# Sliding-window attention and hard-swish MLP: x^T of three pairs by DMA transposes, scores on other banks, and queries in another order

## The chip, the cores and the metric

The kernel runs on one core of a Trainium2 chip. The time is device microseconds of one execution; the median of 8 runs before the change is 320.78 us (319.51 to 322.16). Five engines with a queue each work beside one another: TensorE (PE), VectorE (DVE), ScalarE (ACT), GpSimd (POOL) and SyncE (SP), which here only issues DMAs. Each queue is worked through in order, so an instruction that waits holds up all that stand behind it on its engine.

## What is computed

Attention with 8 batches of 8 heads, 576 tokens and 64 dimensions, where a query sees itself and the 63 keys before it; its output, with the heads side by side, is the input x of 4608 tokens by 512 of two matrix products with a hard-swish between them.

```python
scores = scale * np.matmul(q, k.transpose(0, 1, 3, 2))
rel = pos[:, None] - pos[None, :]
mask = (rel >= 0) & (rel < 64)
attn = softmax(np.where(mask, scores, -1e9))
x = (attn @ v).transpose(0, 2, 1, 3).reshape(B * S, H * D)
h = x @ w_in                               # 4608 x 2048
g = h * np.clip(h + 3.0, 0.0, 6.0) / 6.0
out = g @ w_out                            # 4608 x 512
```

## The kernel before

**Tiles and stages.** The tokens are cut into nine tiles T of 512 for the matrix products, and into eight batches of 576 for attention. A stage is one tile. Its first half, `s1`, computes 16 chunks `fc` of 128 hidden columns: four matmuls (L452) into a PSUM bank, then the gate, an activation on ACT (L459) into a buffer `t` and a product on DVE (L460) into `gT`. Its second half, `s2`, has 16 slots of four matmuls (L489): four token blocks with four slots each, into the banks `o` and `acc` in turn; after the fourth slot of a block ACT copies the bank to `osb` (L495) and SP stores it (L498).

**Attention between the chunks.** In stage T attention of batch T + 1 is put between these, so that x of tile T + 1 is ready. The eight heads go as four pairs g. For a pair:

- `SS` (L551): scores of all key blocks in two PSUM banks `st0`, `st1` (ten matmuls, L347), two exponentials on ACT into `pT` (L355), and one product with the 0/1 mask on DVE, in place (`masked`, L365);
- `N_` (L534): P·V of both heads (L377 to L386), each into an `hT` bank, then for each head a reciprocal and a product on DVE into `opg` (L394, L397), which read that bank;
- `X_` (L539): five PE transposes of `opg` into an `hT` bank (L407) and an ACT copy into `xT` (L412), the x^T that `s1` of the next tile reads.

**What sets the order.** It is written out by hand. `stage_` (L698) runs a chunk or a slot and then the pieces that the tables `p1` (after a chunk of s1) and `p2` (after a slot of s2) of `pieces` (L716) give for its number. In tiles 2 to 6 pair 0's `SS` follows chunk 13, pair 1's slot 0, then `N_(0)` and `SS(2)` slot 3, and so on up to `X_(3)` after slot 14. Each engine receives its part in the order of these calls.

**Buffers.** `hT` has two banks (`ps_h`), which are taken in turn; `st0`, `st1`, `o` and `acc` are one each. `s1_bank` (L421) gives a chunk its bank: before, `hT` for the first two of every four chunks and `st0`/`st1` for the others, up to chunk 11; `o` and `acc` for 12 and 13; `hT` for 14 and 15. A bank is free again when the DVE product of its chunk, or the norm of its head, is done. `t` has three buffers (`t1pool`), `opg` two, and `pT` four.

**Loads and transposes.** `load_for_dma` (L124) brings Q, K and V of batch T + 2 in at the start of stage T, each as five DMAs on SP with rows of 256 bytes (L94). POOL casts them to bf16 (L252, L256, L243 to L247). `transpose_by_dma` (L264), called after slot 6, issues one DMA transpose each for Q and K on SP, into `QT` and `KT`, where a column is a token in order. For batch 2 this is done by pairs (L274), before tile 1. Batches 0 and 1 take another way, which stays.

Of the kernel before, what the change touches and what calls it, by code (L numbers as in the profile page):

```python
# [9 lines left out]
F32 = mybir.dt.float32  # L10
BF16 = mybir.dt.bfloat16
EXP = mybir.ActivationFunctionType.Exp
RELU = mybir.ActivationFunctionType.Relu
MULT = mybir.AluOpType.mult
# [10 lines left out]
def kernel(  # L25
# [9 lines left out]
    nc = tc.nc  # L35
    P = nc.NUM_PARTITIONS
    B, H, S, D = q.shape
# [4 lines left out]
    KB = (S + P - 1) // P  # L42
    SP = KB * P
    R = 4
    SM = P * R
    SR = S - SM
# [4 lines left out]
    QW = P + WINDOW  # L51
    VW = D + 1
    scale = 1.0 / math.sqrt(D)

    consts = ctx.enter_context(tc.tile_pool(name="consts", bufs=1))
    stage = ctx.enter_context(tc.tile_pool(name="stage", bufs=1))
    small = ctx.enter_context(tc.tile_pool(name="small", bufs=4))
    opool = ctx.enter_context(tc.tile_pool(name="opool", bufs=2))
    gpool = ctx.enter_context(tc.tile_pool(name="gT", bufs=1))
    t1pool = ctx.enter_context(tc.tile_pool(name="t1", bufs=3))  # L60
    t2pool = ctx.enter_context(tc.tile_pool(name="t2", bufs=2))
# [1 line left out]
    ps_st = ctx.enter_context(tc.tile_pool(name="ps_st", bufs=1, space=PSUM))  # L63
    ps_o = ctx.enter_context(tc.tile_pool(name="ps_o", bufs=1, space=PSUM))
    ps_h = ctx.enter_context(tc.tile_pool(name="ps_h", bufs=2, space=PSUM))
    ps_acc = ctx.enter_context(tc.tile_pool(name="ps_acc", bufs=1, space=PSUM))
# [56 lines left out]

    def load_for_dma(b):  # L124
        sts, ins = [], []
        for n, src in (("qst", q), ("kst", k), ("vst", v)):
            t = stage.tile([P, KB, H, D], F32, name=n, tag=n)
            ins += load_blocks(t, src, b, range(KB), SR if src is v else 0)
            sts.append(t)
        return tuple(sts), ins  # L130

    ctx.enter_context(tc.manual_schedule())
    def load_first():
# [24 lines left out]
    xT = consts.tile([P, NG, NT + SP - S], BF16, name="xT")  # L158
# [3 lines left out]
    def keep_busy(n):  # L162
# [11 lines left out]
        out=mask1[:], in_=mask1[:], pattern=[[1, QW]], compare_op=ISGE,  # L174
# [3 lines left out]
        out=mask1[:], in_=mask1[:], pattern=[[-1, QW]], compare_op=ISGE,  # L178
        fill=0.0, base=WINDOW - 1, channel_multiplier=1,
    )  # L180
    qn_all = consts.tile([P, NG, KB, 2, D], BF16, name="qn")
# [32 lines left out]
    fill_v(0)  # L214

    mask = consts.tile([P, 2 * (KB - 1), QW], BF16, name="mask")

    win16 = consts.tile([P, NG, FF], BF16, name="win16")
    wout16 = consts.tile([P, NFC, DM], BF16, name="wout16")
# [16 lines left out]
    class Batch:  # L236
# [10 lines left out]
            copy(out=self.V[SR:P, KB - 1, :, 0:D], in_=vst[SR:P, KB - 1, :, :])  # L247

        def cast_for_dma(self, st, which=(0, 1, 2)):
            for n, s in [((qn_all, st[0]), (kn_all, st[1]))[i] for i in which if i < 2]:  # L250
                for g in range(NG):
                    pcopy(  # L252
                        out=n[:, g, 0 : KB - 1, :, :].rearrange("p k h d -> p k (h d)"),
                        in_=s[:, 0 : KB - 1, 2 * g : 2 * g + 2, :].rearrange("p k h d -> p k (h d)"),
                    )
                pcopy(  # L256
                    out=n[:SR, :, KB - 1, :, :].rearrange("p g h d -> p g (h d)"),
                    in_=s[:SR, KB - 1, :, :].rearrange("p (g h) d -> p g (h d)", h=2),
                )
            if 2 in which:  # L260
                self.cast_v(st[2], 0, H, pcopy)
                self.cast_v_end(st[2], pcopy)
# [66 lines left out]
    def scores(bt, g, u, bias=False, bank=None):  # L329


        pT = P_ring[(bt.b * NG + g) % NPT]
        st = ps_st.tile([P, 2, 512], F32, name=f"st{u if bank is None else bank}")
        w = 2 * QW
        if bias:
            for h in range(2):
                nc.tensor.matmul(
                    st[:, h, 0:w], lhsT=ident[:], rhs=maskneg[:, u * w : (u + 1) * w],
                    start=True, stop=False,
                )  # L340
        blocks = (
            ((0, 0, 0, QW), (QW, P, P, QW)),
            ((0, 2 * P, 2 * P, QW), (QW, 3 * P, 3 * P, P), (QW + P, S - P, SM, SR)),
        )[u]
        for o0, k0, q0, n in blocks:
            for h in range(2):
                nc.tensor.matmul(  # L347
                    st[:, h, o0 : o0 + n],
                    lhsT=bt.KT[h * D : (h + 1) * D, g, k0 : k0 + P],
                    rhs=bt.QT[h * D : (h + 1) * D, g, q0 : q0 + n],  # L350
                    start=not bias, stop=not bias or o0 == blocks[-1][0],
                )

        def exps():
            nc.scalar.activation(  # L355
                out=pT[:, :, 2 * u : 2 * u + 2, 0:QW],
                in_=st[:, :, 0:w].rearrange("p h (k w) -> p h k w", k=2),
                func=EXP, scale=scale,
            )

        return exps

    def masked(bt, g):
        pT = P_ring[(bt.b * NG + g) % NPT]
        nc.vector.tensor_tensor(  # L365
            out=pT[:, :, :, 0:QW], in0=pT[:, :, :, 0:QW],
            in1=mask[:].rearrange("p (h k) w -> p h k w", h=2), op=MULT,
        )

    opgs = {}  # L370
# [41 lines left out]
        return lambda: acopy(out=xT[:, g, bt.b * S : (bt.b + 1) * S], in_=tr[:, 0:S])  # L412


    def h_bank():
        return ps_h.tile([P, 512], F32, name="hT")

# [3 lines left out]
    def s1_bank(fc, T):  # L421
        if T == 0:
            if fc in (6, 7):
                return (ps_o, ps_acc)[fc - 6].tile([P, 512], F32, name=("o", "acc")[fc - 6])[:]
            if fc in (8, 9, 12, 13):
                return ps_st.tile([P, 2, 512], F32, name=f"st{fc % 2}")[:, 0, :]
            return h_bank()[:]
        if fc in (12, 13):
            return (ps_o, ps_acc)[fc - 12].tile([P, 512], F32, name=("o", "acc")[fc - 12])[:]
        if fc % 4 < 2:  # L430
            return h_bank()[:]
        return ps_st.tile([P, 2, 512], F32, name=f"st{fc % 2}")[:, 0, :] if fc < 12 else h_bank()[:]
# [130 lines left out]
    bt, st = Batch(0), stage0  # L563
# [152 lines left out]
    def pieces(bt):  # L716
        if bt is None:
            return {}, {}
        f = lambda fn, *a: lambda: fn(bt, *a)
        p1, p2 = {}, {}  # L720
        p1 = {} if bt.b == 2 else {13: [f(SS, 0)]}
        p2 = {
            3: [f(N_, 0), f(SS, 2)], 5: [f(X_, 0)], 6: [f(N_, 1), f(SS, 3)],
            8: [f(X_, 1)], 9: [f(N_, 2)], 11: [f(X_, 2)], 12: [f(N_, 3)], 14: [f(X_, 3)],
        }
        if bt.b == 2:
            p2[0], p2[1] = [f(SS, 0)], [f(SS, 1)]
        else:
            p2[0] = [f(SS, 1)]
        return p1, p2  # L730

    bt2 = Batch(2)
    bt2.cast_for_dma(st2, (0, 1))
    for u0, osb in held:
# [4 lines left out]
    for T in range(1, NTB):  # L739
        p1, p2 = pieces(nxt)  # L740
        b = T + 2
        nxt = None
        if b < B:
            sts, _ = load_for_dma(b)
            nxt = Batch(b)
            p1.setdefault(12 if T == 1 else 6, []).append(
                lambda bt=nxt, sts=sts: bt.cast_for_dma(sts)
            )
            p2.setdefault(6, []).append(lambda bt=nxt: bt.transpose_by_dma())
        stage_(T, None, p1, p2)  # L750


# [28 lines left out]
```

## Time and profile before

Times of one profiled execution, in us. A row of DVE or ACT gives the mean of one instruction.

| what | value |
|---|---|
| time of the profiled execution, its span | 320.5, 318.8 |
| tiles 2 to 6, from start to start (95.5, 128.4, 161.2, 194.1, 227.0, 259.8) | 32.87 each |
| tiles 7 and 8, without attention | 27.63 each |
| PE transposes of x^T, L407 (160) | 14.2 busy |
| product with the mask on DVE, L365 (28) | 1.048, median 0.959 |
| DVE product of a gate, 512 columns, L460 | 0.687 |
| exponentials on ACT, L355 (64) | 0.809 |
| ACT copy of x^T, L412 (32) | 0.640 |
| POOL cast of Q, K of a pair, L252; of V, L243 | 0.66; 1.955 |
| SP's issue of a load at L94; of Q's, K's transpose of a batch, L266 | 1.0 to 1.15; 3.46, 2.80 |
| SP's issue of a pair's transpose, L274; from issue to landing | 1.2; 2.4 to 7.2 |

Busy times of pipelined matmuls overlap, so a matmul's cost is better read from the start of one group to the start of the next. The page's busy line shows PE far ahead of the others. Its DMA line shows the 16 DMA engines at nine tenths or more in most slices up to about 190 us:

```profile
DMA  7899999999899999999969974999100110020011
```

A slice is a fortieth of the span, 8 us. From 224 us on, when all loads are in, little but output stores is left.

### The profile page before, as it was taken

How to read it: one execution, taken by the hardware profiler on the slowest of the kernel's cores; microseconds unless marked ns; L12 is line 12 of the kernel's file. 1: busy time of each engine (PE TensorE's matmuls, PEld its weight loads, DVE VectorE, ACT ScalarE, POOL GpSimd, SP SyncE). 2: the span in 40 equal slices, each digit the busy share in tenths (PEclk: the TensorE clock that was granted, in tenths of full speed). 3: DMA queues.
4: the chain of work that ended last, by engine and by line, in shares of the span. 5: the costliest groups of instructions: out<-in, count | busy, mean ns of one | idle time of the engine just before them, and what ended most of it. 6: DMA issues, size and time to landing. Idle time of an engine off the chain costs nothing.

```text
span 318.8 us, 5760 instructions
## 1 busy us (share of the span) xinstructions
PE 305.9 (96%) x2242; PEld 154.7 (49%) x2242; DVE 177.3 (56%) x331; ACT 188.6 (59%) x280; POOL 85.9 (27%) x131
## 2 busy tenths in 40 slices
PE   7789799998999999999999999999999999999995
PEld 3454445543554455446544564455545554444442
DVE  4568644386636764576547644867477537405700
ACT  3548753387637853785468645874577457417711
POOL 5750805363054143316503530354000000000000
PEclk9999999999999999999999999999999999999999
DMA  7899999999899999999969974999100110020011
GB/s 217 215 182 254 245 202 199 203 202 226 179 206 190 269 206 201 236 221 204 241 187 212 201 190 122 210 205 200 69 0 12 56 67 1 18 82 35 0 67 66
DMA packets 140764, 50.19 MB, mean 157 GB/s; under 512 B 128192, under 2 KB 136384, under 8 KB 140736
## 3 DMA queue, kind: packets, MB, share of 16 engines
q1 hardware_dynamic: 135920, 44.31, 68.7%
q0 software_dynamic: 4544, 5.24, 9.1%
q8 instruction: 17, 0.28, 0.4%
q10 hardware_dynamic: 272, 0.26, 0.2%
q14 instruction: 11, 0.09, 0.1%
HBM read 36.70 MB, written 9.44 MB: 145 GB/s over the span
## 4 chain that ended last, share of the span: by engine, by line
PE 74%; DMA 16%; SPq 6%; POOL 2%; issue 1%; ACT 1%; POOLq 0%
PE acc L489 18%; PE o L489 17%; PE hT L452 15%; PE st L452 11%; PE st L347 3%; DMA wout<-in_moe_w_out_dram 3%; SPq L94 3%; DMA vst<-in_v_dram 3%; DMA win<-in_moe_w_in_dram 3%; DMA KT<-kn 2%; PE hT L407 2%; DMA kst<-in_k_dram 2%; PE acc L452 2%; PE o L452 2%; PE hT L377 2%; DMA rst<-in_k_dram 2%
## 5 line engine op out<-in xcount | busy, mean ns | idle before, releaser
L452 PEld LDWEIGHTS <-win 128*128 128x128 bf16 x576 | 55.7, 98 | 66.8 <-issue 1.0
L489 PEld LDWEIGHTS <-gT 128*128 128x128 bf16 x576 | 52.6, 98 | 55.4 <-issue 0.5
L489 PE MATMUL acc<-wout,gT 128*128 128x512 bf16 x288 | 70.1, 380 | 0.0
L460 DVE SCALAR_TENSOR_TENSOR gT<-t,hT 128x512 bf16<-128x512 bf16 x68 | 46.1, 687 | 42.5 <-ACT t L459 42.4
L489 PE MATMUL o<-wout,gT 128*128 128x512 bf16 x288 | 68.9, 379 | 0.6 <-DMA wout<-in_moe_w_out_dram 0.6
L452 PE MATMUL hT<-xT,win 128*128 128x512 bf16 x272 | 64.5, 379 | 0.0
L355 ACT ACTIVATE pT<-st 128x768 bf16<-128x768 f32 x64 | 48.7, 809 | 17.1 <-PE st L347 17.1
L452 PE MATMUL st<-xT,win 128*128 128x512 bf16 x232 | 55.0, 379 | 0.4 <-DVE gT L460 0.3
L459 ACT ACTIVATE t<-hT,half 128x512 bf16<-128x512 f32 x68 | 46.0, 690 | 10.3 <-PE hT L452 10.3
L460 DVE SCALAR_TENSOR_TENSOR gT<-t,st 128x512 bf16<-128x512 bf16 (+1 forms) x54 | 39.0, 726 | 15.1 <-ACT t L459 15.1
L459 ACT ACTIVATE t<-st,half 128x512 bf16<-128x512 f32 (+1 forms) x54 | 38.6, 718 | 10.3 <-PE st L452 10.1
L365 DVE TENSOR_TENSOR pT<-pT,mask 128x1536 bf16<-128x1536 bf16 x28 | 29.4, 1048 | 19.2 <-ACT pT L355 19.2
L412 ACT COPY xT<-hT 128x576 bf16<-128x576 bf16 x32 | 20.5, 640 | 29.1 <-PE hT L407 29.1
L252 POOL CAST qn<-qst 128x512 bf16<-128x512 f32 x24 | 15.2, 670 | 69.7 <-DMA qst<-in_q_dram 69.7
L495 ACT COPY osb<-o 128x512 f32<-128x512 f32 x18 | 10.5, 586 | 36.8 <-PE o L489 36.8
L397 DVE TENSOR_TENSOR opg<-hT,rec 128x320 bf16<-128x320 f32 x56 | 27.5, 491 | 1.9
L394 DVE RECIPROCAL rec<-hT 128x5 f32<-128x5 f32 x56 | 10.6, 189 | 29.2 <-PE hT L386 29.1
L377 PEld LDWEIGHTS <-pT 128*128 128x128 bf16 x256 | 17.8, 97 | 10.1 <-issue 2.5
L243 POOL CAST V<-vst 128x512 bf16<-128x512 f32 (+1 forms) x14 | 16.7, 1191 | 17.8 <-DMA vst<-in_v_dram 17.1
L347 PE MATMUL st<-QT,KT 64*128 64x192 bf16 (+2 forms) x320 | 17.9, 229 | 3.0 <-ACT KT L316 1.5
L252 POOL CAST kn<-kst 128x512 bf16<-128x512 f32 x24 | 14.8, 656 | 18.7 <-DMA kst<-in_k_dram 18.7
L495 ACT COPY osb<-acc 128x512 f32<-128x512 f32 x18 | 10.6, 588 | 14.6 <-PE acc L489 14.6
(76 smaller groups left out, 234.8 us busy)
## 6 DMA issues: line engine op xcount, KB each, us to landing
out_dram<-osb SPq DMA_DIRECT2D x32, 256.0 KB, 2.3
qst<-in_q_dram SPq DMA_DIRECT2D x28, 256.0 KB, 4.7
kst<-in_k_dram SPq DMA_DIRECT2D x27, 256.0 KB, 5.3
vst<-in_v_dram SPq DMA_DIRECT2D x24, 256.0 KB, 5.3
vst<-in_v_dram SPq DMA_DIRECT2D x24, 128.0 KB, 4.3
win<-in_moe_w_in_dram POOLq DMA_DIRECT2D x4, 512.0 KB, 7.7
wout<-in_moe_w_out_dram POOLq DMA_DIRECT2D x4, 512.0 KB, 8.6
qst<-in_q_dram SPq DMA_DIRECT2D x2, 512.0 KB, 5.4
```

What stands on the lines that cost most here:

```text
L252: pcopy(out=n[:, g, 0 : KB - 1, :, :].rearrange("p k h d -> p k (h d)"), in_=s[:, 0 : KB - 1, 2 * g : 2 * g + 2, :].rearrange("p k h d -> ...
L347: nc.tensor.matmul(st[:, h, o0 : o0 + n], lhsT=bt.KT[h * D : (h + 1) * D, g, k0 : k0 + P], rhs=bt.QT[h * D : (h + 1) * D, g, q0 : q0 + n], ...
L355: nc.scalar.activation(out=pT[:, :, 2 * u : 2 * u + 2, 0:QW], in_=st[:, :, 0:w].rearrange("p h (k w) -> p h k w", k=2), func=EXP, scale=scale,
L365: nc.vector.tensor_tensor(out=pT[:, :, :, 0:QW], in0=pT[:, :, :, 0:QW], in1=mask[:].rearrange("p (h k) w -> p h k w", h=2), op=MULT,)
L377: nc.tensor.matmul(ob, lhsT=pT[:, h, qb, 0:P], rhs=V[:, qb, 2 * g + h, :], start=True, stop=(qb == 0),)
L397: nc.vector.tensor_tensor(out=opgs[bt.b, g][:, :, h, :], in0=ov[:, :, 0:D], in1=rec[:].unsqueeze(2).to_broadcast([P, KB, D]), op=MULT,)
L412: return lambda: acopy(out=xT[:, g, bt.b * S : (bt.b + 1) * S], in_=tr[:, 0:S])
L452: nc.tensor.matmul(hT, lhsT=win16[:, g, fc * P : (fc + 1) * P], rhs=xT[:, g, t0 : t0 + TB], start=(g == 0), stop=(g == NG - 1),)
L459: nc.scalar.activation(out=t1[:], in_=hT, func=RELU, bias=half[:], scale=1.0 / 6.0)
L460: nc.vector.scalar_tensor_tensor(out=out, in0=t1[:], scalar=1.0, in1=hT, op0=MIN, op1=MULT,)
L489: nc.tensor.matmul(accs[ts], lhsT=gT[:, fc, ts * P : (ts + 1) * P], rhs=wout16[:, fc, :], start=(fc == 0), stop=(fc == NFC - 1),)
L495: nc.scalar.copy(out=osb[:], in_=accs[ts])
```

## The change

1. `X_` of pairs 0 to 2 of batches 3 to 7 becomes `xt_dma`: one DMA transpose on SP's queue from `opg` into `xT`, without PE or ACT. It writes 640 columns, the last 64 of which the next batch writes over. Pair 3 stays on PE. `opg` gets four buffers.
2. For these batches the tables move. `SS(0)` and `SS(1)` now follow chunks 10 and 14 of s1, `SS(2)` slot 0, `N_(0)` slot 1, `SS(3)` slot 3, `N_(1)`, `N_(2)` and `N_(3)` slots 4, 7 and 10, and `X_(3)` slot 12. Batch 2 keeps its order.
3. From tile 2 on, chunks 0 and 1 of s1 take `st0` and `st1`, and the others take `hT` (third and fourth of four) and `o`/`acc` (first and second), so that the score banks are free from chunk 2 on.
4. The transposes of Q and K of the next batch are called after slot 12 instead of slot 6, from tile 2 on.
5. Q of batches 2 to 7 is loaded with four tokens to a partition: two DMAs of four heads with rows of 1 KB and one for the last 64 tokens. A column of `QT` is then no longer a token in order: the 512 tokens lie as four groups j of 128. The scores read QT in that order (the number and width of the matmuls stays: 192, 128 and 64 columns), the exponentials go into a new buffer `raw` (two of them) in the same order, and the mask product reads `raw` and a mask `maskj` of that order and writes `pT` in order of tokens, which makes its output step four elements.

```diff
-    opool = ctx.enter_context(tc.tile_pool(name="opool", bufs=2))
+    rawp = ctx.enter_context(tc.tile_pool(name="raw", bufs=2))
+    opool = ctx.enter_context(tc.tile_pool(name="opool", bufs=4))
...
     def load_for_dma(b):
-        for n, src in (("qst", q), ("kst", k), ("vst", v)):
+        for h0 in range(0, H, 4):
+            ins.append(nc.sync.dma_start(
+                out=qst[:, h0 : h0 + 4, :],
+                in_=q[b, h0 : h0 + 4, 0:SM, :].rearrange("h (p j) d -> p h (j d)", j=R),
+            ))
+        ins.append(nc.sync.dma_start(
+            out=rst[0:SR, :, :], in_=q[b, :, SM:S, :].rearrange("h s d -> s h d"),
+        ))
+        for n, src in (("kst", k), ("vst", v)):
...
         def cast_for_dma(self, st, which=(0, 1, 2)):
+                        pcopy(
+                            out=n[:, g, 0 : KB - 1, :, :],
+                            in_=st[0][0][:, 2 * g : 2 * g + 2, :].rearrange("p h (j d) -> p j h d", j=R),
+                        )
...
     def scores(bt, g, u, bias=False, bank=None):
+        if bt.b > 1:
+            for i in range(2):
+                for h in range(2):
+                    kb = 2 * u + i
+                    n = min(QJ, P - kb * P // R)
+                    nc.tensor.matmul(
+                        st[:, h, i * QW : (i + 1) * QW].rearrange("p (j s) -> p j s", j=R)[:, :, 0:n],
+                        lhsT=bt.KT[h * D : (h + 1) * D, g, kb * P : (kb + 1) * P],
+                        rhs=bt.QT[h * D : (h + 1) * D, g, 0:SM].rearrange("d (j s) -> d j s", j=R)[
+                            :, :, kb * P // R : kb * P // R + n
+                        ],
+                        start=True, stop=True,
+                    )
...
+            return lambda: nc.scalar.activation(
+                out=raw[:, :, 2 * u : 2 * u + 2, :],
+                in_=st[:, :, 0:w].rearrange("p h (k w) -> p h k w", k=2),
+                func=EXP, scale=scale,
+            )
...
     def masked(bt, g):
+        if bt.b > 1:
+            nc.vector.tensor_tensor(
+                out=pT[:].rearrange("p h k (s j) -> p (h k) j s", j=R)[:, :, :, 0 : QW // R],
+                in0=raws.pop((bt.b, g))[:].rearrange("p h k (j s) -> p (h k) j s", j=R),
+                in1=maskj[:], op=MULT,
+            )
+            return
...
+    def xt_dma(bt, g):
+        opg = opgs.pop((bt.b, g))
+        t0 = bt.b * S
+        nc.sync.dma_start_transpose(
+            out=xT[:, g, t0 : t0 + SP].rearrange("d (k s) -> d k s", s=P),
+            in_=opg[:].rearrange("p k h d -> p (k h d)"),
+        )
...
     def s1_bank(fc, T):
+        if T > 1 and fc < 2:
+            return ps_st.tile([P, 2, 512], F32, name=f"st{fc}")[:, 0, :]
+        if T > 1:
+            if fc % 4 > 1:
+                return h_bank()[:]
+            return (ps_o, ps_acc)[fc % 4].tile([P, 512], F32, name=("o", "acc")[fc % 4])[:]
...
     def pieces(bt):
-        p1 = {} if bt.b == 2 else {13: [f(SS, 0)]}
+        p1 = {10: [f(SS, 0)], 14: [f(SS, 1)]}
         p2 = {
-            3: [f(N_, 0), f(SS, 2)], 5: [f(X_, 0)], 6: [f(N_, 1), f(SS, 3)],
-            8: [f(X_, 1)], 9: [f(N_, 2)], 11: [f(X_, 2)], 12: [f(N_, 3)], 14: [f(X_, 3)],
+            0: [f(SS, 2)], 1: [f(N_, 0)], 3: [f(SS, 3), f(xt_dma, 0)], 4: [f(N_, 1)],
+            6: [f(xt_dma, 1)], 7: [f(N_, 2)], 9: [f(xt_dma, 2)], 10: [f(N_, 3)], 12: [f(X_, 3)],
         }
-            p2[0] = [f(SS, 1)]
...
+    nc.vector.tensor_copy(out=maskj[:], in_=mask[:].rearrange("p n (s j) -> p n j s", j=R))
...
-            p2.setdefault(6, []).append(lambda bt=nxt: bt.transpose_by_dma())
+            p2.setdefault(6 if T == 1 else 12, []).append(lambda bt=nxt: bt.transpose_by_dma())
```

## The prediction

> **What bounds the kernel now.** I read the page's busy line and chain of waits first, then the timelines of TensorE (PE), ScalarE (ACT) and VectorE (DVE) over one steady stage, then the groups by form and the DMA queue's timeline. From the page:
>
> ```profile
> PE 305.9 (96%) x2242; PEld 154.7 (49%) x2242; DVE 177.3 (56%) x331; ACT 188.6 (59%) x280; POOL 85.9 (27%) x131
> ...
> PE 74%; DMA 16%; SPq 6%; POOL 2%; issue 1%; ACT 1%; POOLq 0%
> ```
>
> PE is busy nearly always, and the DMA and SPq shares of the chain lie before 77 us. From there on the chain in order of time is PE alone. So in tiles 2 to 6 (95.5 to 259.8 us, five stages of 32.87 us) every PE instruction removed is time gained, and every PE stall added is time lost. The PE timeline of tile 5, columns start, duration, instruction:
>
> ```profile
> 205.17 1.03 PE L452 MATMUL acc<-xT,win 128*128 128x512 bf16 x4
> 206.13 0.51 PE L347 MATMUL st<-QT,KT 64*128 64x192 bf16 x10
> 206.56 1.90 PE L452 MATMUL hT<-xT,win 128*128 128x512 bf16 x8
> ...
> 215.06 0.44 PE L407 MATMUL hT<-ident,opg 128*128 128x128 bf16 x5
> 215.34 1.03 PE L489 MATMUL acc<-wout,gT 128*128 128x512 bf16 x4
> 216.20 0.22 PE L377 MATMUL hT<-V,pT 128*128 128x65 bf16 x2
> ```
>
> Reading start to start: one s1 chunk or s2 slot of four matmuls takes 0.864 us (twelve chunks from 193.94 to 204.30); a pair's scores take 0.54 (the last matmuls end near 206.03, the next start at 206.56); x^T of a pair 0.28 (215.06 to 215.34); P·V of a pair 0.48 (216.20 to 216.68), half of it, 0.24, a head. The stage adds up: 32 x 0.864 + 4 x (0.54 + 0.48 + 0.28) = 32.84. PE waits for nobody in it. Before it, in tile 1, there is one stall:
>
> ```profile
> 76.87 0.51 PE L347 MATMUL st<-QT,KT 64*128 64x192 bf16 x10 [0.91 <-DMA KT<-kn]
> ```
>
> The other engines' steps, ACT first (same stage):
>
> ```profile
> 206.23 0.69 ACT L459 ACTIVATE t<-acc,half 128x512 bf16<-128x512 f32 x1 [0.18 <-PE acc L452]
> 206.82 1.50 ACT L355 ACTIVATE pT<-st 128x768 bf16<-128x768 f32 x2
> 208.20 1.28 ACT L459 ACTIVATE t<-hT,half 128x512 bf16<-128x512 f32 x2
> ```
>
> ```profile
> 208.35 0.96 DVE L365 TENSOR_TENSOR pT<-pT,mask 128x1536 bf16<-128x1536 bf16 x1 [0.71 <-ACT pT L355]
> 209.23 1.28 DVE L460 SCALAR_TENSOR_TENSOR gT<-t,hT 128x512 bf16<-128x512 bf16 x2
> ...
> 214.81 2.69 DVE L365 TENSOR_TENSOR pT<-pT,mask 128x1536 bf16<-128x1536 bf16 x1 [0.71 <-ACT pT L355]
> 217.42 0.18 DVE L394 RECIPROCAL rec<-hT 128x5 f32<-128x5 f32 x1
> ```
>
> An ACT gate holds its engine 0.59 (206.23 to 206.82); two exponentials end 1.50 after they start; the mask starts 0.03 later (208.32 to 208.35) and holds DVE 0.88 (to 209.23). A DVE gate takes 0.69. ACT starts a gate about 0.20 after its matmuls end. A pair's normalisation takes 1.33 (217.42 to 218.75). PE resumed 0.05 after a DVE gate that it waited for (begun at 64.76 and 1.217 long, so 65.98, to 66.03).
>
> **What the Trainium skill says.** "VectorE: DVE Perf Modes", section "What auto-detection actually checks": two 16-bit results a cycle need every tensor, the output too, at step 1 or -1. The present mask has that, and its 1536 elements in 0.96 us agree. The new mask writes pT at a step of 4 elements, so by this page it gets one a cycle. The trace has that rate in the gate, which reads fp32:
>
> ```profile
> L460 DVE SCALAR_TENSOR_TENSOR gT<-t,st 128x1024 bf16<-128x1024 bf16 x4 | 4.7, 1217 | 7.0 <-ACT t L459 7.0
> ```
>
> With 0.687 us for 512 elements, one element costs (1217 - 687) / 512 = 1.035 ns and an instruction 0.157 us. "SBUF — State Buffer", section "Who interferes with whom": a DVE instruction with two SBUF inputs and a GpSimd instruction that reads SBUF shut each other out for a whole instruction. The trace agrees: the mask of 2.69 us above began with this one, and took 1.73 more than its usual 0.96:
>
> ```profile
> 214.80 1.90 POOL L243 CAST V<-vst 128x2048 bf16<-128x2048 f32 x1 [2.06 <-DMA vst<-in_v_dram]
> ```
>
> **The change part by part.** The sum stands against the profiled execution, 320.5 us (span 318.8 and 1.7 around it), which is 0.28 under the median of the runs.
>
> 1. x^T of pairs 0 to 2 leaves PE in five stages (batches 3 to 7): 15 x 0.28 = -4.2 us. ACT loses 15 copies of 0.64, which covers nothing, since ACT had slack. Each becomes a DMA transpose of five blocks on SP's queue; the like instruction (L274) takes SP 1.2 us and lands 2.4 to 7.2 us after issue, 3.6 in the median. The last of the three has its input some 6 slots before the stage's end, 5 us or more: it lands in time at the median; at the slowest it would cost up to 2 us a stage. I take nothing. Behind it on SP wait an output store, Q's and K's transposes and the next loads.
>
> 2. Those transposes move from slot 6 to slot 12. They hold SP about 3.5 and 2.8 us and have landed some 8 us into the next stage. Pair 0's scores need them after chunk 10, 11 x 0.864 = 9.5 us in. The next loads start 3 us later than now and Q issues 3 us faster (point 4), so the casts come where they came. Nothing.
>
> 3. The masks. At 1.035 ns an element a mask lasts 0.157 + 1536 x 1.035 ns = 1.75 us and holds DVE 1.67 instead of 0.88. Below, it could stay at 0.88; I take 1.67. Whether this is hidden is read from what stands behind it in DVE's queue. Two places of a stage decide.
>
> First, pairs 0 and 1 in s1. From the end of chunk 10: ACT gate 10, 0.20 + 0.59; exponentials 1.50; mask 0, 0.03 + 1.67; gate 11 of DVE 0.69; then ACT's gate 14, 0.05 + 0.59, since the t buffers are three and 14 takes that of 11; exponentials of pair 1, 1.50; mask 1, 0.03 + 1.67; gate 15, 0.69; 0.05. Sum 9.26 us. Only then is chunk 15's hT bank free, and P·V of pair 0, head 1, now at slot 1, takes that bank. PE would be there after scores 0, chunks 11 to 14, scores 1, chunk 15, slot 0, scores 2, slot 1 and head 0: 3 x 0.54 + 7 x 0.864 + 0.24 = 7.91. PE stalls 1.35 us. With the old mask the chain is 7.68, and there is no stall.
>
> Second, from the end of slot 3: output copy on ACT 0.20 + 0.48, exponentials of pair 3 1.50, mask 3 0.03 + 1.67, the norms of pair 1 behind it 1.33, 0.05: 5.26. PE reaches P·V of pair 2, head 1, which needs pair 1's second bank, after scores 3, slot 4, pair 1, slots 5 to 7, head 0: 0.54 + 0.864 + 0.48 + 2.59 + 0.24 = 4.71. Stall 0.55; with the old mask 4.47, none.
>
> So 1.90 us per stage, 9.5 in five. In tile 1 the order is the old one, with P·V of pair 0 two slots later, and no bank comes late: nothing there, though the masks are slow.
>
> 4. Q by three loads instead of five for batches 2 to 7. SP takes about 1.1 us for each 256 KB piece at L94 (1024 short rows) and 0.5 for 512 KB at L107 (rows of 1 KB): 3 us less issue. That shortens the way to batch 2's KT, for which PE waited 0.91 in tile 1; a lead of 1 us is enough: -0.9 (bounds 0 and -1.1). Later it only feeds casts that have slack. For batch 3, pair 0's scores come three chunks earlier (2.6 us) than now, where KT landed 0.6 ahead (106.93, used at 107.53); the lead of SP should be about 3: between 0 and +1, I take +0.2.
>
> 5. Masks against casts. The mask still has two SBUF inputs. In four stages POOL casts about 8.9 us of 32.9 (27%). Three masks a stage now lie on PE's path; each meets a cast with that chance and waits half of one, 0.3 to 0.95: 3 x 0.27 x 0.45 = 0.36 a stage, 1.5 in four. Bounds: 0, and 3 a stage (two short casts of 0.6 and the V cast of 1.9).
>
> 6. maskj's copy, once, 1 to 2 us: DVE is idle from 60.5 to 64.8 there, so nothing; without that cover, 2 us. The other banks in s1 keep the distance of four chunks between uses: nothing. The strided tail of the scores has 64 columns: under 0.05 us a pair; nothing.
>
> Sum: -4.2 + 9.5 - 0.9 + 0.2 + 1.5 = +6.1. 320.5 + 6.1 = 326.6, and with the 0.28 to the median 326.9.
>
> **Rivals.** A, faster: DVE absorbs the masks. For it speaks that DVE is busy only 56%; against it that both places are queues behind one instruction, where average slack is no help. The deciding quantity is the mask's hold d: the stalls come to (2d - 1.99) + (d - 1.12), which equals the gain of 0.84 + 0.9/5 a stage at d = 1.38 us. Below that the change wins; at 0.88 it gives 320.8 - 4.2 - 0.9 = 315.7. Chance 0.12.
>
> B, only the first place stalls, and casts miss the masks: 5 x (1.35 - 0.84) - 0.9 = +1.7, 322.5, with 320 to 324 around it. For it speaks that the second stall is a difference of 0.55 between two long sums. 0.12.
>
> C, collisions each stage: pair 3's mask behind the V cast, another behind a short one, 2.2 us instead of 0.36, or x^T landing late: 326.9 + 4 x 1.84 = 334, with 330 to 335. The V cast does fall about 21 us into a stage, near mask 3 at 23. 0.10.
>
> The forecast itself, both places stalling, 323.5 to 330: 0.66.
>
> **How the numbers follow.** 326.9 is the likeliest case. 320.0 to 331.5 takes in the forecast, B and about half of C; A and the rest of C, 0.17, lie outside. The forecast's own range is 323.5 to 330. Beyond 0.3% (about 1 us, what runs can tell) lie: faster, A and a sliver of B, 0.13; within, 0.04 of B; slower, the rest, 0.83.
>
> **What would show it.** The mask's mean near 1.75 us (step 3; under 1.4 makes the prediction wrong). PE waiting for a DVE gate at P·V of pair 0 and for the norms at pair 2, together near 1.9 us a stage, stages near 34 us from tile 2 to 6, 27.6 for tiles 7 and 8. 75 fewer L407 matmuls, and no KT wait near 76 us. Any PE wait for the x^T transposes would add to the forecast; no waits for DVE on PE would refute it.

## The result, and the profile after

The changed kernel takes 368.55 us in the median (365.7 to 371.4, 11 runs) against 320.5 us (32 runs) for the kernel before: ratio 1.1482, 95% interval 1.1449 to 1.1515. The forecast was 326.9 us with a range to 331.5. The direction was right; the loss is 48 us where 6 were forecast.

In the code after, the mask product is L419, a gate L533 (ACT) and L534 (DVE), s1 and s2 matmuls L526 and L563, P·V L437 to L446, its normalisation L454 and L457, x^T on PE L467, and the POOL casts of K and V L269 and L256. From the page of the changed kernel: the busy line, the chain of work that ended last, and two groups of instructions (count, busy us, mean ns, idle before).

```profile
PE 314.4 (86%) x2167; PEld 151.4 (41%) x2167; DVE 239.3 (65%) x332; ACT 177.9 (49%) x265; POOL 125.7 (34%) x131
...
PE 48%; DVE 30%; DMA 9%; ACT 7%; issue 3%; SPq 2%; POOL 1%; ACTq 0%; POOLq 0%
...
L419 DVE TENSOR_TENSOR pT<-raw,maskj 128x1536 bf16<-128x1536 bf16 x24 | 92.6, 3868 | 7.0 <-ACT raw L389 7.0
...
L269 POOL CAST kn<-kst 128x512 bf16<-128x512 f32 x24 | 27.4, 1178 | 20.1 <-DMA kst<-in_k_dram 20.1
```

PE has 75 instructions fewer, as the change says, and yet its busy share has fallen from 96% to 86%: it waits. DVE, which the chain of before did not contain, holds 30% of the chain now. The mask took 0.96 us before and lasts 3.87 us on average, at least 3.58. The cast of K went from 0.66 to 1.18.

By stages (length, then busy time of PE, its weight loads, DVE, ACT and POOL with the count of instructions in brackets, then the share of its full clock that PE was granted, the DMA share and GB/s), tiles 2 to 6 of the changed kernel, each 32.87 us before:

```profile
100.79:144.03 43.24, 36.22 (x239) 17.03 (x238) 31.62 (x36) 19.29 (x29) 22.03 (x16) 0.92 0.78 157
144.03:184.78 40.75, 34.60 (x239) 16.38 (x238) 30.37 (x36) 19.29 (x29) 21.13 (x13) 0.96 0.85 158
184.78:226.19 41.41, 34.45 (x238) 16.55 (x237) 31.04 (x36) 19.18 (x29) 15.01 (x13) 0.96 0.72 155
226.19:266.99 40.80, 33.21 (x238) 15.97 (x237) 30.42 (x36) 19.17 (x29) 18.17 (x13) 1.00 0.74 158
266.99:306.57 39.58, 33.22 (x239) 15.96 (x238) 29.19 (x36) 19.18 (x29) 0.00 (x0) 1.00 0.31 65
```

The last of them, tile 6, is the cleanest: no POOL cast and full clock. It is 39.58 - 32.87 = 6.71 us longer than before. Its PE timeline, the first three lines with a wait (idle before the instruction, and the releaser):

```profile
282.96 1.02 PE L526 MATMUL hT<-xT,win 128*128 128x512 bf16 x4 [1.82 <-DVE gT L534]
289.27 0.22 PE L437 MATMUL hT<-V,pT 128*128 128x65 bf16 x2 [2.55 <-DVE gT L534]
293.34 0.24 PE L437 MATMUL hT<-V,pT 128*128 128x65 bf16 x2 [0.51 <-DVE opg L457]
```

And DVE in the same stretch:

```profile
285.12 3.58 DVE L419 TENSOR_TENSOR pT<-raw,maskj 128x1536 bf16<-128x1536 bf16 x1 [0.43 <-ACT raw L389]
288.51 0.71 DVE L534 SCALAR_TENSOR_TENSOR gT<-t,hT 128x512 bf16<-128x512 bf16 x1
289.15 3.59 DVE L419 TENSOR_TENSOR pT<-raw,maskj 128x1536 bf16<-128x1536 bf16 x1
292.53 0.21 DVE L454 RECIPROCAL rec<-hT 128x5 f32<-128x5 f32 x1
```

The wait of 1.82 us is that of chunk 15 for the gate of chunk 11, which stands behind pair 0's mask. The gate of chunk 15 (begun at 288.51) stands behind pair 1's mask, and PE's P·V of pair 0, head 1, at 289.27 waits for the bank that this gate gives back. Both belong to the first place that the prediction named. Its second, P·V of pair 2, waits 1.03 and 0.21 us for norms behind pair 3's mask. Between them lies a place that it did not name: pair 0's norms (292.53) stand behind pair 2's mask, and P·V of pair 1 waits for them at 293.34 for 0.51 us and once more for 0.21. A mask holds DVE for 288.51 - 285.12 = 3.39 us.

Of the 47.2 us that the profiled span grew (318.8 to 366.0), five times tile 6's 6.71 are 33.5. Tiles 2 to 5 lie 3.66, 1.17, 1.83 and 1.22 above tile 6, together 7.9. Tile 1 grew from 35.25 to 40.10, 4.85. Tiles 7 and 8 are unchanged at 27.62. The remaining 0.9 lies before tile 1 and at the end.

### The profile page after: what moved, and what is told of

Its sections match the earlier page's. It is cut to its first block, busy times and chain, and to the rows that moved or that the text cites. A ratio compares the mean times of both kernels' runs of the same rounds, so it can differ in the third digit from the quotient of the medians.

```text
span 366.0 us, 5611 instructions
## 1 busy us (share of the span) xinstructions
PE 314.4 (86%) x2167; PEld 151.4 (41%) x2167; DVE 239.3 (65%) x332; ACT 177.9 (49%) x265; POOL 125.7 (34%) x131
## 4 chain that ended last, share of the span: by engine, by line
PE 48%; DVE 30%; DMA 9%; ACT 7%; issue 3%; SPq 2%; POOL 1%; ACTq 0%; POOLq 0%
DVE pT L419 23%; PE acc L563 11%; PE o L563 11%; PE hT L526 9%; PE st L526 5%; ACT raw L389 5%; PE acc L526 4%; PE o L526 4%; DVE opg L457 3%; DVE gT L534 3%; DMA win<-in_moe_w_in_dram 2%; DMA rst<-in_k_dram 2%; ACT t L533 2%; DMA wout<-in_moe_w_out_dram 2%; DMA qst<-in_q_dram 1%
## 5 line engine op out<-in xcount | busy, mean ns | idle before, releaser
L419 DVE TENSOR_TENSOR pT<-raw,maskj 128x1536 bf16<-128x1536 bf16 x24 | 92.6, 3868 | 7.0 <-ACT raw L389 7.0
L526 PEld LDWEIGHTS <-win 128*128 128x128 bf16 x576 | 55.7, 98 | 76.1 <-issue 10.5
L563 PEld LDWEIGHTS <-gT 128*128 128x128 bf16 x576 | 53.9, 99 | 61.0 <-issue 6.0
L526 PE MATMUL hT<-xT,win 128*128 128x512 bf16 x272 | 66.6, 381 | 9.5 <-DVE gT L534 9.5
L563 PE MATMUL o<-wout,gT 128*128 128x512 bf16 x288 | 72.3, 393 | 0.7 <-DMA wout<-in_moe_w_out_dram 0.6
L563 PE MATMUL acc<-wout,gT 128*128 128x512 bf16 x288 | 69.5, 383 | 0.0
L533 ACT ACTIVATE t<-hT,half 128x512 bf16<-128x512 f32 x68 | 46.6, 689 | 21.4 <-DVE gT L534 12.7
L534 DVE SCALAR_TENSOR_TENSOR gT<-t,st 128x512 bf16<-128x512 bf16 (+1 forms) x26 | 19.7, 769 | 51.2 <-ACT t L533 51.2
L534 DVE SCALAR_TENSOR_TENSOR gT<-t,hT 128x512 bf16<-128x512 bf16 x68 | 46.9, 692 | 9.2 <-ACT t L533 9.0
L274 POOL CAST qn<-qst 128x512 bf16<-128x512 f32 x24 | 20.4, 881 | 79.9 <-DMA qst<-in_q_dram 79.9
L437 PE MATMUL hT<-V,pT 128*128 128x65 bf16 x224 | 18.9, 198 | 26.5 <-DVE opg L457 14.0
L389 ACT ACTIVATE raw<-st 128x768 bf16<-128x768 f32 x48 | 36.2, 813 | 4.5 <-PE st L372 4.5
L269 POOL CAST kn<-kst 128x512 bf16<-128x512 f32 x24 | 27.4, 1178 | 20.1 <-DMA kst<-in_k_dram 20.1
L437 PEld LDWEIGHTS <-pT 128*128 128x128 bf16 x256 | 17.6, 99 | 40.2 <-DVE opg L457 20.0
L526 PE MATMUL st<-xT,win 128*128 128x512 bf16 x120 | 28.6, 379 | 0.6 <-DVE gT L534 0.3
L457 DVE TENSOR_TENSOR opg<-hT,rec 128x320 bf16<-128x320 f32 x56 | 27.5, 491 | 2.2
L526 PE MATMUL o<-xT,win 128*128 128x512 bf16 x92 | 23.6, 379 | 0.0
L526 PE MATMUL acc<-xT,win 128*128 128x512 bf16 x92 | 23.6, 379 | 0.0
L454 DVE RECIPROCAL rec<-hT 128x5 f32<-128x5 f32 x56 | 10.7, 192 | 18.6 <-PE hT L446 18.5
L533 ACT ACTIVATE t<-st,half 128x512 bf16<-128x512 f32 (+1 forms) x26 | 19.4, 752 | 6.0 <-PE st L526 5.9
```

What stands on the lines that cost most here:

```text
L269: pcopy(out=n[:, g, 0 : KB - 1, :, :].rearrange("p k h d -> p k (h d)"), in_=st[1][:, 0 : KB - 1, 2 * g : 2 * g + 2, :].rearrange("p k h d ...
L274: pcopy(out=n[:, g, 0 : KB - 1, :, :], in_=st[0][0][:, 2 * g : 2 * g + 2, :].rearrange("p h (j d) -> p j h d", j=R),)
L389: return lambda: nc.scalar.activation(out=raw[:, :, 2 * u : 2 * u + 2, :], in_=st[:, :, 0:w].rearrange("p h (k w) -> p h k w", k=2), func= ...
L419: nc.vector.tensor_tensor(out=pT[:].rearrange("p h k (s j) -> p (h k) j s", j=R)[:, :, :, 0 : QW // R], in0=raws.pop((bt.b, g))[:].rearran ...
L437: nc.tensor.matmul(ob, lhsT=pT[:, h, qb, 0:P], rhs=V[:, qb, 2 * g + h, :], start=True, stop=(qb == 0),)
L454: nc.vector.reciprocal(out=rec[:].unsqueeze(2), in_=ov[:, :, D:VW])
```

## The experiments

**What the product costs (p_prices).** The kernel before with a list of DVE instructions put at its end, each form twice: the same product of 1536 bf16 elements, with the output at steps of 1, 2, 3, 4 and 8 elements, the new mask's own form, strided inputs, and an fp32 output. Only their durations are read.

```diff
+        tt(O, A)
+        tt(step(X, 2, n), A)
+        tt(step(X, 3, n), A)
+        tt(step(X, 4, n), A)
+        tt(step(X, 8, n), A)
...
+        tt(O, step(X, 4, n))
...
+        tt(f32[:, 0:n], A)
+        tt(step(f32, 2, 768), A[:, 0:768], M[:, 0:768])
```

> The kernel before, with a list of VectorE instructions after its last stage, each twice, on data that nobody reads; its time says nothing, the rows do. Every product has 1536 elements of bf16 with the mask as second input unless said. Outputs at steps 1, 2, 3, 4 and 8; output in the new mask's form of 8 x 4 x 48 with step 4, and the same form with step 1; first input at step 4 with a contiguous output; inputs in inner rows of 4 at step 48 with a contiguous output; an fp32 output, contiguous and (768 elements) at step 2; 768 elements at steps 1 and 4; copies with step 4 on the output and on the input. Theory W (the write step costs): 0.96 us at step 1, 3.4 to 3.6 at every output step from 2 on whatever the form, 1.75 for strided inputs, 1.75 for the contiguous fp32 output. Rival F (the form of 32 short rows costs): 1.75 for the plain steps and 3.6 only for the two forms of 8 x 4 x 48. Rival R (any product at one element a cycle from two SBUF inputs costs this): 3.6 for strided inputs and the fp32 output as well.

Groups of that kernel by form, in windows of its end (busy us, mean ns). The first five are outputs at step 1, 2, 3, 4 and 8; then come the input at step 4 with a dense output, the fp32 output at step 1, and the fp32 output at step 2 with 768 elements:

```profile
L730 DVE TENSOR_TENSOR pT<-pT,mask 128x1536 bf16<-128x1536 bf16 x2 | 1.9, 955 | 0.0
L730 DVE TENSOR_TENSOR xT<-pT,mask 128x1536 bf16<-128x1536 bf16 x2 | 3.8, 1879 | 0.0
L730 DVE TENSOR_TENSOR xT<-pT,mask 128x1536 bf16<-128x1536 bf16 x2 | 5.5, 2740 | 0.1
L730 DVE TENSOR_TENSOR xT<-pT,mask 128x1536 bf16<-128x1536 bf16 x2 | 7.1, 3566 | 0.1
L730 DVE TENSOR_TENSOR xT<-pT,mask 128x1536 bf16<-128x1536 bf16 x2 | 13.9, 6953 | 0.1
L730 DVE TENSOR_TENSOR pT<-xT,mask 128x1536 bf16<-128x1536 bf16 x2 | 3.5, 1759 | 0.1
L730 DVE TENSOR_TENSOR kst<-pT,mask 128x1536 f32<-128x1536 bf16 x2 | 3.5, 1752 | 0.0
L730 DVE TENSOR_TENSOR kst<-pT,mask 128x768 f32<-128x768 bf16 x2 | 1.9, 960 | 0.1
```

The bf16 output of 768 elements at step 4, and then, as shortest, median and longest ns, the new mask's own form (rows of 48 at step 4):

```profile
L730 DVE TENSOR_TENSOR xT<-pT,mask 128x768 bf16<-128x768 bf16 x2 | 3.7, 1858 | 0.0
```

```profile
L730 DVE TENSOR_TENSOR pT<-pT,mask x2: 3573/3680/3786, 334.8 to 338.6; 128x1536 bf16<-128x1536 bf16 x2
```

The time of a bf16 output grows with its step: each further element of step adds 0.83 to 0.92 us, (6.953 - 3.566) / 4 = 0.85 from 4 to 8. That is 0.55 ns for each of the 1536 elements and each element of step, as if the gaps were walked through too. Theory W had expected one price for every step from 2 on, which is not so. The short rows are not the cause (rival F): the same 8 x 4 x 48 form at step 1 took 0.96 us. Nor is it any slow product from two SBUF inputs (rival R): one input at step 4 costs 1.76 us, what the prediction took for any stride, and so does an fp32 output. Both inputs in rows of 4 at a step of 48, though, took 2.74. An fp32 output at step 2 has the same distance in bytes as a bf16 one at step 4, yet takes only 0.96 for 768 elements, where the bf16 output at step 4 took 1.86. So it is neither the distance in bytes nor "a stride" as such. The operation counts too: a copy of 1536 elements with its output at step 4 took 1.87 us, half the product's time. Why the engine takes this time stays open.

**The mask without its stride (e1_mask_step1).** The changed kernel, whose mask writes `pT` in `raw`'s order. P·V then takes the queries of a block in another order than it should, so the output is not the reference's; the work is the same.

```diff
-                out=pT[:].rearrange("p h k (s j) -> p (h k) j s", j=R)[:, :, :, 0 : QW // R],
-                in0=raws.pop((bt.b, g))[:].rearrange("p h k (j s) -> p (h k) j s", j=R),
-                in1=maskj[:], op=MULT,
+                out=pT[:, :, :, 0:QW],
+                in0=raws.pop((bt.b, g))[:],
+                in1=maskj[:].rearrange("p (h k) j s -> p h k (j s)", h=2), op=MULT,
```

> The changed kernel, but the mask product writes pT at step 1 in the order of raw, so P.V takes the queries of each 192 in another order than it should and the output is not the reference's; all else, data and instruction counts, stays. Theory M (the mask's hold of VectorE is the whole loss): mask back at 0.96 us, no PE wait for the gate at pair 0 or for the norms at pair 2, stages of tiles 2 to 6 near 32.0 us, time 314 to 318. Rival D (the x^T transposes, the loads or the casts come late, and the mask only stands beside it): stages stay above 36 us, time above 340.

317.57 us, ratio 0.9871 (0.9826 to 0.9917). The mask's mean is 1.008 us, and tiles 3 to 6 take 32.13 to 32.21. The whole loss hangs on this one access pattern, and the rest of the change gains 1.3%. One wait is left in tile 2, 1.11 us for batch 3's KT at the new, earlier place of pair 0's scores.

**The mask at the price that the prediction took (e6_mask_fp32).** As e1, with `maskj` in fp32, which makes the product last 1.75 us.

```diff
-    maskj = consts.tile([P, 2 * (KB - 1), R, QW // R], BF16, name="maskj")
+    maskj = consts.tile([P, KB - 1, R, QW // R], F32, name="maskj")
```

> The run with the mask at step 1 (queries in another order, output not the reference's), but the mask operand is fp32, so that the product runs at one element a cycle: 1.75 us, the very price that the prediction used. If its two chains are right, PE stalls about 1.35 us at pair 0 (in part already at chunk 15) and 0.55 at pair 2 in each of tiles 2 to 6, which makes 9.5 us more than with the mask at step 1, 327 us, up to 328.5 with collisions with casts. If the chains are wrong (average slack of VectorE absorbs it), 317 to 319; if other waits count, above 331.

331.0 us, ratio 1.0319 (1.0271 to 1.0366): more than the 327 to 328.5 expected. The profiled stages of tiles 1 to 6 are 34.35, 34.00, 35.76, 35.23, 35.06 and 34.00. So at 1.75 us the prediction's stage holds where the casts do not meet the masks (33.93 by its sum, 34.00 in tiles 2 and 6), and tile 1 loses nothing. How the two places come out is read against e1, the same kernel with a fast mask. The start of tile 6, the slot after pair 0's P·V and the slot after pair 2's, in e1 and then in e6:

```profile
224.64 1.89 PE L526 MATMUL st<-xT,win 128*128 128x512 bf16 x8
...
242.38 1.89 PE L563 MATMUL o<-wout,gT 128*128 128x512 bf16 x8
...
249.09 2.75 PE L563 MATMUL o<-wout,gT 128*128 128x512 bf16 x12
```

```profile
234.46 1.89 PE L526 MATMUL st<-xT,win 128*128 128x512 bf16 x8
...
253.26 0.22 PE L437 MATMUL hT<-V,pT 128*128 128x65 bf16 x2 [0.81 <-DVE gT L534]
...
253.50 1.89 PE L563 MATMUL o<-wout,gT 128*128 128x512 bf16 x8
...
260.79 2.75 PE L563 MATMUL o<-wout,gT 128*128 128x512 bf16 x12
```

Up to the first slot e6 takes 19.04 us where e1 takes 17.74, so it loses 1.30 (1.35 forecast); from there to the second 7.29 against 6.71, a loss of 0.58 (0.55 forecast). Together they make the 34.00 - 32.13 = 1.87 us of the stage. The waits that the timeline prints come to only 1.02; starts are the safer reading.

Tiles 3, 4 and 5 lie 1.76 + 1.23 + 1.06 = 4.1 us above tile 6, where the prediction had 1.5 for collisions. In each of them pair 3's mask, beside the cast of V, lasts 3.22, 2.98 and 2.82 us in place of 1.75, and P·V of pair 2 waits for the norms behind it, here in tile 3:

```profile
155.62 0.23 PE L437 MATMUL hT<-V,pT 128*128 128x65 bf16 x2 [1.47 <-DVE opg L457]
```

This is the collision that the prediction's rival C described, pair 3's mask behind the V cast. The clock is 1.00 throughout e6, so it is not the clock.

**No casts beside the masks (e7_no_casts).** The changed kernel without POOL's casts of batches 4 to 7, whose attention then works on older data.

```diff
         def cast_for_dma(self, st, which=(0, 1, 2)):
+            if self.b > 3:
+                return
```

> The changed kernel without the GpSimd casts of batches 4 to 7 (their Q, K and V are loaded, but attention works on older data, so the output is not the reference's). If the masks' collisions with casts make tiles 2 to 5 longer than tile 6 (43.2, 40.8, 41.4 and 40.8 against 39.6 us), all five come to 39.6 and the time to about 361. If loads or transposes make them longer, they stay and so does the time, 366 to 370.

362.94 us, a single time. Tiles 2 to 6 take 40.49, 40.02, 39.58, 40.92 and 40.92. Against the changed kernel's tiles 2 to 5 this saves 5.2 us, an estimate of what casts and masks cost each other. It is not a clean one: the clock was at half for some 3.4 us four times in those tiles of the changed kernel (0.92 is two times, 0.96 one), and three times in e7's. The other 2.7 of the 7.9 above tile 6 is still there without casts, so not all five stages came to the 39.6 expected. By the windows it goes with the clock: of these five stages the one at clock 1.00 takes 39.58, the same as tile 6 above, and the four at 0.96 take 40.0 to 40.9. In the changed kernel's tile 2, POOL and DVE show how the casts are held up. First POOL's rows, then DVE's mask:

```profile
119.14 8.50 POOL L269 CAST kn<-kst 128x512 bf16<-128x512 f32 x4 [1.56 <-DMA kst<-in_k_dram]
...
128.15 1.89 POOL L256 CAST V<-vst 128x2048 bf16<-128x2048 f32 x1
```

```profile
127.88 5.59 DVE L419 TENSOR_TENSOR pT<-raw,maskj 128x1536 bf16<-128x1536 bf16 x1
```

Four casts of K, 0.66 us each when alone, take 8.50 us together while masks run (at 118.93 and 122.95), and the mask issued at 127.88 beside the V cast takes 5.59 instead of 3.58.

**The reorder in other places (e3, e4, e8).** Three ways to have tokens in order without a strided DVE output. e3: PE writes the scores to PSUM in token order, at a step of 4 fp32 elements, and there is no `raw`. e4: the mask reads `raw` at a step of 48 in rows of 4 and writes densely. e8: PE reads `QT` in token order instead.

```diff
 e3
-                        st[:, h, i * QW : (i + 1) * QW].rearrange("p (j s) -> p j s", j=R)[:, :, 0:n],
+                        st[:, h, i * QW : (i + 1) * QW].rearrange("p (s j) -> p j s", j=R)[:, :, 0:n],
 e4
-                in0=raws.pop((bt.b, g))[:].rearrange("p h k (j s) -> p (h k) j s", j=R),
+                in0=raws.pop((bt.b, g))[:].rearrange("p h k (j s) -> p (h k) s j", j=R),
 e8
-                        rhs=bt.QT[h * D : (h + 1) * D, g, 0:SM].rearrange("d (j s) -> d j s", j=R)[
-                            :, :, kb * P // R : kb * P // R + n
+                        rhs=bt.QT[h * D : (h + 1) * D, g, 0:SM].rearrange("d (j s) -> d s j", j=R)[
+                            :, kb * P // R : kb * P // R + n, :
```

> The changed kernel, but TensorE puts the scores back in token order as it writes them to PSUM (fp32 at a step of 4 within each 192 columns), the exponentials go straight into pT and the old mask product in place follows; no raw, no maskj. Theory M: 314 to 318, as the run with the mask at step 1, if the strided PSUM write costs TensorE nothing; scores 0.54 us a pair. If TensorE writes strided columns at half speed, scores take 0.3 us more a pair, 1.3 a stage, time 321 to 324. Rival D: above 340.

> The changed kernel, but the mask product takes its first input at a step of 48 in inner rows of 4 and writes pT in token order at step 1 (both inputs in that form, mask in place of maskj). If a strided input costs one element a cycle, the mask takes 1.75 us and this is the case that the prediction worked out: 324 to 330. If it costs as the strided output does (3.6 us), 360 to 372. Rival D: above 340 with a mask of 1.75 us.

> The run where TensorE restores the order, but by reading QT at a step of 128 elements in inner rows of 4 instead of writing PSUM at a step of 4; the PSUM write is contiguous. If the moving operand may be read at any step for nothing, scores go back to 0.54 us a pair and the time to 317 to 318.5, with the right output; if a strided read costs what the strided write cost, 324 to 326.

e3: 325.22 us, ratio 1.0118 (1.0066 to 1.0169). e4: 349.96, ratio 1.0881 (1.0807 to 1.0955), its mask 2.95 us. e8: 337.51, ratio 1.0543 (1.0488 to 1.0598). Groups by form on PE from 100 to 280 us, the scores of 192 columns, in the kernel before, e3 and e8 in this order:

```profile
L347 PE MATMUL st<-QT,KT 64*128 64x192 bf16 x120 | 8.4, 246 | 0.0
```

```profile
L367 PE MATMUL st<-QT,KT 64*128 64x192 bf16 x120 | 13.2, 354 | 0.0
```

```profile
L367 PE MATMUL st<-QT,KT 64*128 64x192 bf16 x120 | 22.8, 494 | 0.0
```

A matmul pays for the stride on either side: its mean is 0.11 us more for a PSUM output at step 4, 0.25 more for a strided moving operand. As matmuls overlap, the cost is read from the stage: tile 6 takes 33.20 us in e3 and 35.55 in e8 against 32.13 in e1, so 0.27 and 0.86 more for a pair. e3 comes out just above the 324 that half speed was to give. e4's mask, with both inputs strided, lies between its two expectations of 1.75 and 3.6, and e8 is slower than either of its own, up to 326. Each of these reorders costs more than x^T on PE did, 0.84 a stage. All three are better than the change as made, none is better than before.

**Part 5 alone (e11_q_only_old_places).** The kernel before with Q's loads, `raw` and the strided mask, all at the old places, x^T on PE.

> The kernel before with only the part on Q (loads of four tokens to a partition, scores in that order, mask with output at a step of 4), at the old places and with x^T on PE. Theory: the mask of 3.6 us alone makes the loss, wherever it stands; in the old order the norms of a pair stand behind the mask of the next, and x^T and P.V wait for them, by my count of DVE's queue about 5 us a stage in tiles 1 to 6, with casts and the lowered clock some 7: 350 to 370. Rival: the new places are what exposes it (masks of pairs 0 and 1 ahead of s1's gates), and in the old places most of it is hidden: tiles 2 to 6 within 2 us of 32.9, 325 to 335.

358.78 us, ratio 1.1184 (1.1129 to 1.1238). Its list of PE's waits (us in total, times, longest) names another place, x^T on PE:

```profile
PE hT L467 <- DVE opg L457: 24.4, 16, 3.6
```

The norms stand behind the masks and x^T on PE waits for them, as in tile 1 of the changed kernel, where the old order is kept: PE waits 1.42 us there for the first mask and 1.68, 0.80 and 1.16 for the norms, 5.06 together. So the moved places are not what makes the mask dear: it costs 38 us at the old ones. They do make it dearer: from e1 to the changed kernel, at the new places, it costs 51 (a difference across series).

**The change without part 5 (e5_q_in_order).** Q's old load, scores and mask; parts 1 to 4 stay.

> The changed kernel without its fifth part: Q is loaded as before, scores and mask are those of before, no raw, no maskj; x^T by DMA, the other banks, the new places and the later Q/K transposes stay. Theory M (the loss is the mask's form alone, the rest gains): as the run with the mask at step 1, 316 to 318.5. If the Q loads in 1 KB rows are worth the 0.9 us of the prediction, this is 0.9 slower than that run; if K's loads give the lead back, within 0.5 of it. Rival D (the places and transposes lose by themselves): above 321.

320.74 us, ratio 1.0009 (0.9984 to 1.0035): a miss. Four of the five stages are where they should be, tiles 3 to 6 at 32.03 to 32.07, so x^T by DMA gives its 0.84 a stage. Tile 2 takes 36.58, with this line (from the list of PE's waits) and a clock of 0.95 in its window:

```profile
PE st L347 <- DMA KT<-kn: 2.6, 2, 2.2
```

The wait is 2.24 us, at pair 0's scores after chunk 10, which were three chunks later before. The stage lost another 2.3 us, and its granted clock was 0.95 against 1.00 in the next four. The profiled execution was 1.9 us above the median of its runs; as its tile 1 begins 1.8 us later than in the kernel before (61.88 against 60.09), this need not lie in tile 2.

**Batch 3 later (e9_batch3_late), then x^T alone (e10_xt_dma_only).** e9 is e5 with batch 3's scores at the old places and its x^T still by DMA. e10 is the kernel before with x^T of pairs 0 to 2 by DMA and nothing moved.

```diff
 e10
+            p2[5], p2[8], p2[11] = [f(xt_dma, 0)], [f(xt_dma, 1)], [f(xt_dma, 2)]
```

> The change without its part on Q (old load, scores and mask), as in e5, but batch 3 keeps its scores at the old places (pair 0 at chunk 13 of s1 instead of 10), while batches 4 to 7 keep the new ones. Theory: what e5 lost is one wait of 2.2 us for batch 3's KT in tile 2 and the lowered clock behind it; that stage took 36.6 us where the four after it took 32.05. With the wait gone the stage takes 32.1 too, and the median comes to about 316 us, ratio 0.987. Rival: the DMA transposes of x^T or the start of the kernel cost the rest, and it stays within 0.3% of before, about 320.

> The kernel before with x^T of pairs 0 to 2 by DMA transposes from batch 3 on, all places, banks and the next batch's transposes (slot 6) as before. Theory of the change's author's order (the moved places are needed, since on SP's queue the transpose of pair 1 stands behind the next batch's Q and K transposes of slot 6, 6 us, and that of pair 2 is issued only at slot 11, about 4 us before the next stage): PE waits for xT at the start of tiles 3 to 6 for 1 to 4 us a stage, total 321 to 335. Rival: these transposes land in time anyway, and the time is 320.5 - 4.2 = 316.3.

e9: 320.73 us, ratio 0.9997 (0.9973 to 1.0021), not the 316 expected. Batch 3's KT is in time, and instead tile 3 waits 3.07 us for x^T. e10: 330.16, ratio 1.0292 (1.0231 to 1.0353). In e10 SP's queue shows why, and below it PE at the start of tile 3:

```profile
119.48 5.33 SPq L94 DMA_DIRECT2D vst<-in_v_dram  x5
...
125.57 1.33 SPq L418 DMA_TRANSPOSE xT<-opg  x1
127.01 2.85 SPq L266 DMA_TRANSPOSE QT<-qn  x1
129.95 2.74 SPq L266 DMA_TRANSPOSE KT<-kn  x1
...
133.42 1.24 SPq L418 DMA_TRANSPOSE xT<-opg  x1
```

```profile
136.12 0.58 PE L460 MATMUL hT<-xT,win 128*128 128x512 bf16 x1 [6.04 <-DMA xT<-opg]
```

The three transposes stand behind the 15 loads of batch 4, which hold SP up to 124.8, and two of them (133.42 and one at 135.37) also behind the next batch's Q and K transposes at slot 6. In e9 the loads end at 123.4, and the first x^T transpose goes out at 124.19.

**Batch 3 as before, the new places from batch 4 on (e12_from_batch4).** e5 with one more branch:

```diff
+        if bt.b == 3:
+            return {13: [f(SS, 0)]}, {
+                0: [f(SS, 1)], 3: [f(N_, 0), f(SS, 2)], 5: [f(X_, 0)],
+                6: [f(N_, 1), f(SS, 3)], 8: [f(X_, 1)], 9: [f(N_, 2)], 11: [f(X_, 2)],
+                12: [f(N_, 3)], 14: [f(X_, 3)],
+            }
```

> The change without its part on Q, as in e5, but batch 3 is left wholly as before (scores at the old places, x^T on PE); batches 4 to 7 have x^T of pairs 0 to 2 by DMA and the new places. In e5 tile 2 waited for batch 3's KT, in e9 tile 3 waited 3.1 us for batch 3's x^T, whose transposes stood on SP behind the 16 loads of batch 4; tiles 3 to 6 of e5 took 32.05 us each against 32.87. Theory: with batch 3 left as before both waits are gone, tile 2 takes 32.9 and tiles 3 to 6 take 32.05: 320.6 - 3.3 = 317.3, ratio 0.990. Rival: another transfer on SP comes late in its place, or the earlier transposes push tile 3, and the time is 319.5 to 321.

318.1 us against 321.08 in the same series, ratio 0.9927 (0.9902 to 0.9953). No wait for KT or xT is left on PE; tile 2 takes 32.86 and tiles 3 to 6 take 32.23, 32.04, 32.04 and 32.03. This version beats both kernels, the one before by 0.7%.

## Why the prediction was right in sign and wrong in size

**Step 3, the price of the mask, is the term that failed.** The prediction put it as "At 1.035 ns an element a mask lasts 0.157 + 1536 x 1.035 ns = 1.75 us and holds DVE 1.67 instead of 0.88. Below, it could stay at 0.88; I take 1.67." The mask lasted 3.58 us and held DVE 3.39. The rate came from the gate, an instruction that reads fp32 and has a dense output; an fp32 operand alone takes a dense mask from 0.96 to 1.75 us (e6). The Trainium skill, "VectorE: DVE Perf Modes", section "What auto-detection actually checks", says that a step other than 1 or -1 loses the faster mode; the prediction read this as one element a cycle at any step. The measurement decides otherwise: 2.2 ns an element at step 4. An fp32 input is a different reason for slowness than a strided bf16 output, and the step of 4 did not enter the sum at all. The prediction names no row of before with such an output, so the cost above was unknown, and it bounded it only from below. Its range therefore had no room for what came.

**The two chains held.** e6, at the price assumed, loses 1.30 and 0.58 us at the two places, where the prediction had 1.35 and 0.55. With 3.39 in its own formula they are 2 x 3.39 - 1.99 = 4.79 and 3.39 - 1.12 = 2.27. From e1 to the changed kernel tile 6 loses 4.78 up to the slot after pair 0's P·V (22.52 us against 17.74), then 1.08 up to the slot after pair 1's and 1.59 up to that after pair 2's, 7.45 in all. So the first place comes out as worked, and part of the second place's loss falls on pair 1, which the prediction did not name; at 1.75 us pair 1 loses nothing.

**"Nothing there" in tile 1 was wrong.** It holds at 1.75 us (e6) and not at 3.58: the norms queue behind the masks, and tile 1 lost 4.85 us. The statement had been worked out for one duration only.

**Step 5, collisions,** was 1.5 us in four stages. e6 shows 4.1 even at 1.75, and e7 about 5.2 at 3.58, inside the bound of 3 a stage. The average share of POOL's cast time understates this: the casts come in blocks at the places where the masks stand, and in e6 the V cast met pair 3's mask in three stages of four, as rival C had it, and cost 1.06 to 1.76 us a stage instead of its 2.2. The lowered clock after waits, about 2.7 us of tiles 2 to 5 by e7, was in no term.

**Step 1** was right, 0.84 us a stage in e5 and e12. "It lands in time", however, rested on the other parts: e10 shows 10.4 us of waits for xT without the moved places. **Step 2**, "nothing", was right as a cost, and hid that the move to slot 12 takes 6 us of transposes out of the way of x^T.

**Step 4**, the gain from Q's faster loads, is not shown. Tile 1 gained 0.9 in e6 as forecast and 0.5 in e1, but also 1.1 in e9 and 1.0 in e12 (34.14 and 34.27), which keep Q's old loads; with the old loads PE's wait for KT there ranges from nothing (e9, e12) to 1.7 us (e10). So the agreement in e6 may be luck. For batch 3's KT the prediction took +0.2 with a bound of +1; at the new place PE waits 2.24 with the old loads (e5), and 1.11 (e1) or nothing (e6) with the new ones. That the faster issue helps there is likely, from one trace each.

Rival A gave 315.7 for a mask that holds DVE as before, and e1 measured 317.57, of which 1.1 is the KT wait of tile 2. Its argument, that DVE's slack absorbs a slower mask, is refuted by e6.

## What to carry to other kernels

Take a rate from a row that is slow for the same cause; if the trace has no such row, the upper bound stays open and belongs in the range. When one instruction grows on an engine with slack, list what stands behind it in that engine's queue and work the stall out as a function of the duration, in every stage: the formula survived here where the number fell. And a DMA put on a shared queue stands behind the loads ahead of it (15 of them in e9 and e10), so parts of a change that look independent (x^T, places, Q's loads) must be costed together on that queue.

## What was not expected of the hardware

- A DVE product with a bf16 output of 1536 elements took 0.955, 1.879, 2.740, 3.566 and 6.953 us at steps of 1, 2, 3, 4 and 8; a copy at step 4 took 1.87. An fp32 output at step 2 took 0.96 for 768 elements, against 1.75 for 1536 dense ones.
- A score matmul of 192 columns had a mean of 0.246 us dense, 0.354 with PSUM written at step 4 and 0.494 with its moving operand read in rows of 4 at a step of 128.
- After waits of PE the granted clock was lower in some stages: 0.92 to 0.96 over a stage, 0.57 in the four us from 116.8 of the changed kernel. The Trainium skill, "TensorE: Matmul & The Clock Gate", section "What's actually happening", says of the clock that "the default state is throttled, and activity releases the throttle". The trace agrees in kind: the kernel before, whose PE does not wait there, has 1.00 in its tiles 2 to 6. In e7 it cost 0.4 to 1.3 us a stage; its third stage, with much the same waits, stayed at 1.00. What decides between them was not tried.
